# Later blocks' attention bias made by POOL instead of ACT, and the first two weight pieces decoded behind the sixth and seventh pair's exponentials

## The chip, the cores and the metric

The kernel runs on one core of one Trainium2 chip. The metric is device time in microseconds (us), lower is better. Three timed runs of the kernel before gave 570.25, 571.13 and 571.83 us, median 571.13 us. One further execution was profiled; every duration below comes from that one.

The engines are PE (TensorE, matmuls; PEld is its weight load), DVE (VectorE), ACT (ScalarE), POOL (GpSimd) and SP (SyncE, which issues all the DMAs here). Each works through its own instructions in a fixed order and waits for the others by semaphores.

## The reference

Attention with 8 heads of 64 over two batches of 768 tokens, then two dense blocks on the 512-wide result. In the attention every token sees the first few tokens and its own last 96, with a bias that grows with distance, by a slope of its own in each head:

```
scores = q @ k.T / sqrt(D)
dist = where(is_global & ~is_local, n_local, abs(rel))
scores = scores - slopes[h] * dist ; scores = where(keep, scores, -1e9)
a = exp(scores - max) / (sum + 1e-9) ; x = a @ v
x = x + relu(layernorm(x) @ w_ch1) @ w_ch2          # 512 -> 2048 -> 512
theta = x @ w_theta ; y = w_tok_r @ (x cos theta) + w_tok_i @ (x sin theta)
u = x + y ; out = u + relu(u @ w_ch)
```

All inputs are float32 or 64-bit; the weights come in a 64-bit packing and are turned into float32 on the chip ("decoded"), and then split in a high and a low part for the matmuls.

## The kernel before, in words

The 1536 tokens are 12 blocks of 128 rows, taken in the order 0, 6, 1, 2, 3, 4, 5, 7 to 11. Blocks 0 and 6 are the first of their batch: they see only their own 128 columns. Every later block sees a window of 256 columns: 96 earlier ones, 32 for the global tokens, its own 128.

A step of the attention is one pair of heads of one block (four steps to a block). `scores` (L184) gives PE two score matmuls `s`, DVE adds the bias and takes the maximum (L204, tiles `e` and `nm`), and ACT takes the exponential with its sum (L211). Two steps later `flip_probs` transposes `e` on PE into `pt` (L221) and copies it out to `pts`: by ACT for the second and third pair of a block (L224), by DVE for the other two (L226). Three steps later `values` multiplies `pts` with v into `xa` (L240). Six to eight steps later `finish_x` copies `xa` (ACT, L250), transposes it (`xp`, L255) and scales it (DVE, L256), `layer_norm` works on it (DVE and POOL, L268 to L277), and `make_xt` transposes the result (`xnp`, L284). In the first two blocks `spin` puts matmuls of zeros between the steps.

The bias tiles, one of 128 x 384 for each head, are made by `make_bias` (L119) in two parts: `first`, the 128 columns of blocks 0 and 6, and `old`, the 256 columns of all later blocks. DVE builds the distance once (`bias_rel`), and it is scaled once for each head: `first` by DVE (L150), `old` by ACT (L148). The first user of `old` is the third block.

The dense weights come in 58 pieces of 128 x 512. `load_to` (L298) queues the 512 KB load of a packed piece (`raw`) on SP into one of three buffers; `decode` (L306) takes a first approximation on ACT (L314) and three steps on DVE (L322 to L324), and queues the load that may use the buffer next. `split_w` decodes two pieces and makes their high parts on ACT and their low parts on POOL (L340, L341).

The instructions are traced in the order of the code (L768 to L828); a scheduler then settles each engine's order by its own estimate of what is ready first. `tc.issue_after(x)` holds what it encloses, on the engine of x, behind x in that order; it adds no wait for x to end. Around the change the code traces four attention steps, then `split_w(0)` with the first two pieces, then the other steps (L787 to L795). `behind_maximum` (L116) uses `issue_after` for DVE.

Of the kernel before, what the change touches and what calls it, by code (L numbers as in the profile page):

```python
# [8 lines left out]
F32 = mybir.dt.float32  # L9
# [4 lines left out]
AF = mybir.ActivationFunctionType  # L14
ALU = mybir.AluOpType
# [17 lines left out]
def kernel(ctx, tc, q, kwin, v, n_pair, g_ln, wall, out):  # L33
    nc = tc.nc
# [15 lines left out]
    SCALE = 1.0 / D**0.5  # L50
# [13 lines left out]
    def ps(tag, shape, name):  # L64
        return bank(tag, shape, name, BANKS[tag])

    def spin(tag, name, n):

        o = ps(tag, [P, DM], name)
        for _ in range(n):  # L70
            nc.tensor.matmul(o, zero[:, 0:P], zero, start=True, stop=True)
# [11 lines left out]
    def load_n():  # L83
        low = keep.tile([P, 2], F32, name="low")
        nc.vector.tensor_copy(low, words.bitcast(U32)[:, :, 0])
        nc.vector.scalar_tensor_tensor(nval, words[:, :, 1], 2.0**32, low, ALU.mult, ALU.add)
# [24 lines left out]
    nc.vector.memset(zero, 0.0)  # L111
    bias = [at.tile([P, WIN + P], BF16, name=f"bias{h}") for h in range(H)]

    maxima = []

    def behind_maximum(n):  # L116
        return tc.issue_after(maxima[n]) if n is not None else ExitStack()

    def make_bias():  # L119

        n = WIN + P
        rel, key, a = (at.tile([P, n], F32, tag="xn", name=f"bias_{x}", bufs=3) for x in ("rel", "key", "a"))
        io = dict(allow_small_or_imprecise_dtypes=True)
        v_ = nc.vector
        own = rel[:, P:n].rearrange("p (t c) -> p t c", c=P)
        old, first = slice(0, WIN), slice(WIN, n)
        nc.gpsimd.iota(own, [[0, 2], [-1, P]], base=0, channel_multiplier=1, **io)
        nc.gpsimd.iota(key[:, first], [[1, P]], base=0, channel_multiplier=0, **io)
        nc.gpsimd.iota(rel[:, 0:PREV], [[-1, PREV]], base=PREV, channel_multiplier=1, **io)
        nc.gpsimd.iota(key[:, PREV:P], [[1, GLOB]], base=0, channel_multiplier=0, **io)  # L130
        v_.memset(rel[:, PREV:P], FAR)
        v_.memset(key[:, 0:PREV], FAR)
        v_.memset(key[:, P:WIN], FAR)
        v_.tensor_scalar(a[:, P:n], rel[:, P:n], 0.0, FAR, ALU.is_lt, ALU.mult)
        v_.tensor_tensor(rel[:, P:n], rel[:, P:n], a[:, P:n], ALU.max)
        yield
        load_n()
        for part in (first, old):
            r, k_, a_ = rel[:, part], key[:, part], a[:, part]
            with behind_maximum(3 if part is old else None):  # L140
                v_.tensor_scalar(a_, r, nl, NEG, ALU.is_ge, ALU.mult)
                v_.tensor_scalar(k_, k_, ng, NEG, ALU.is_ge, ALU.mult)
            v_.tensor_tensor(r, a_, r, ALU.subtract)
            v_.scalar_tensor_tensor(r, k_, nl, r, ALU.subtract, ALU.max)
            for h in range(H):
                slope = 2.0 ** (-8.0 * (h + 1) / H)
                if part is old:
                    nc.scalar.activation(bias[h][:, part], r, AF.Copy, scale=slope / SCALE)  # L148
                else:
                    v_.tensor_scalar(bias[h][:, part], r, slope / SCALE, None, ALU.mult)  # L150
            yield

    def slot(name):
# [30 lines left out]
    def scores(b, i, p, startup):  # L184
        nk = WIN if i else P
        b0 = 0 if i else WIN
        if p == 0:
            stat[b, i] = (
                at.tile([P, H], F32, tag="nm", name=f"nm{b}_{i}", bufs=2),
                at.tile([P, H], F32, tag="sm", name=f"sm{b}_{i}", bufs=2),  # L190
            )
        nm, sm = stat[b, i]
        qb, kb = qt[b, i], kt[b, i]
        s = [ps("h" if startup and p % 2 else "s", [P, nk], f"s{b}_{i}_{p}_{j}") for j in range(2)]
        k0 = WIN - nk
        for j in range(2):
            rows = slice(j * D, (j + 1) * D)
            nc.tensor.matmul(s[j], qb[rows, p, :], kb[rows, p, k0:WIN], start=True, stop=True)  # L198
        if startup:
            spin("o", f"spin{b}_{p}", 2)  # L200
        e = at.tile([P, 2, nk], F32, tag="p", name=f"e{b}_{i}_{p}", bufs=3)
        for j in range(2):
            h = 2 * p + j
            r = nc.vector.tensor_tensor_reduce(  # L204
                out=e[:, j, :], in0=s[j], in1=bias[h][:, b0:b0 + nk], scale=-SCALE, scalar=3.0e38,
                op0=ALU.add, op1=ALU.min, accum_out=nm[:, h:h + 1],
            )
            maxima.append(r.ins)
        for j in range(2):
            h = 2 * p + j  # L210
            nc.scalar.activation(e[:, j, :], e[:, j, :], AF.Exp, bias=nm[:, h:h + 1], scale=-1.0, accum_out=sm[:, h:h + 1])  # L211
        e_t[b, i, p] = e

    def flip_probs(b, i, p, startup):
# [83 lines left out]
    def load_to(n):  # L298
        while n_staged[0] <= min(n, len(order) - 1):
# [3 lines left out]
            stage[i] = r  # L303
            n_staged[0] += 1

    def decode(i, out):  # L306

        n = n_decoded[0]
        n_decoded[0] += 1
        load_to(n)  # L310
        assert order[n] == i
        r = stage.pop(i)
        load_to(n + NRAW)
        nc.scalar.activation(out, r.bitcast(F32)[:, :, 1], AF.Copy, scale=2.0**-112)  # L314
        t = rawp.tile([P, DM], I32, tag="dec", name=f"dec{i}", bufs=1)
        o = out.bitcast(I32)
        if i >= 4 * GROUP:
            nc.scalar.activation(t, r.bitcast(U32)[:, :, 0], AF.Copy, scale=2.0**-29 * (1 - 2.0**-15), bias=-0.4999)
            nc.vector.scalar_tensor_tensor(t, o, 3, t, ALU.logical_shift_left, ALU.bitwise_or)
            nc.vector.scalar_tensor_tensor(o, r[:, :, 1], -2**31, t, ALU.bitwise_and, ALU.bitwise_or)  # L320
            return
        nc.vector.tensor_scalar(t, o, 3, None, ALU.logical_shift_left)  # L322
        nc.vector.scalar_tensor_tensor(t, o, -2**31, t, ALU.bitwise_and, ALU.bitwise_or)
        nc.vector.scalar_tensor_tensor(o, r[:, :, 0], 29, t, ALU.logical_shift_right, ALU.bitwise_or)  # L324
# [273 lines left out]


    def general():  # L600
        es = ExitStack()
        ga = es.enter_context(tc.tile_pool(name="ga", bufs=1))
        row = ga.tile([P, S], F32, name="g_row")
# [5 lines left out]
        for b in range(B):  # L609
# [3 lines left out]
            for i in range(NQ):  # L613
# [6 lines left out]
                v_ = nc.vector  # L620
# [11 lines left out]
                for h in range(H):  # L632
                    n_ = f"{t}_{h}"
                    e = ga.tile([P, S], F32, tag="e", name=f"g_e{n_}", bufs=2)
                    st_ = ga.tile([P, 3], F32, tag="st", name=f"g_st{n_}", bufs=2)
                    slope = 2.0 ** (-8.0 * (h + 1) / H)
# [82 lines left out]
        for t in range(NTT):  # L719
            o = tmp(f"g_o{t}")  # L720
            nc.vector.scalar_tensor_tensor(o, product(flip(x2[t], f"g_u{t}"), CH, f"g_ch{t}"), 0.0, x2[t], ALU.max, ALU.add)
            b, i = divmod(t, NQ)
# [56 lines left out]
    def steps_to(n):  # L779
        while n_step[0] < n:  # L780
            next(st, None)
            n_step[0] += 1
# [6 lines left out]
    next(bias_steps)  # L789
    load_to(1)  # L790
    nc.sync.dma_start(gbc, g_ln.partition_broadcast(P))
    steps_to(4)
    split_w(0)
    steps_to(done_at(0))
    split_w(1)  # L795
# [75 lines left out]
    with tc.If(nc.values_load(slow[0:1, 0:1], min_val=0, max_val=1, skip_runtime_bounds_check_because="0 or 1") > 0):  # L871
        general()
# [49 lines left out]
```

## Time and profile before

| | |
|---|---|
| timed runs, median (lowest to highest) | 571.13 us (570.25 to 571.83) |
| profiled execution, its whole time | 572.38 us |
| its span, first to last instruction | 570.5 us |
| PE busy in the span | 555.1 us (97%) |
| DVE, ACT, POOL busy | 365.7, 282.7, 121.9 us |
| granted TensorE clock, mean | 0.998 |

The profiled execution took 1.25 us more than the median of the timed runs. PE is busy nearly throughout; an engine's idle time matters only where PE waits for it. The attention of the first blocks fills about the first 60 us, and from there on matmuls of the dense block stand between the attention's steps. Stretches are read from a view that gives each engine's busy time in a window, and waits from a timeline that names, in brackets, how long an engine sat idle before an instruction and what ended that.

### The profile page before, as it was taken

The page shows a single profiled execution, that of the slowest core. Times are in us where ns is not written, and L with a number is a line of the kernel's source. Part 1 is how long each engine was busy: PE and PEld are TensorE (multiplying, and loading weights), DVE is VectorE, ACT ScalarE, POOL GpSimd, SP SyncE. Part 2 cuts the span into 40 slices and gives each one's busy share as a digit, 9 for nine tenths or more (in the row PEclk, how much of TensorE's full clock was granted, in tenths as well). Part 3 has the DMA queues.
Part 4 walks back from the last instruction along what each step waited for, and adds up shares of the span by engine and source line. Part 5 has one row for each costly group of instructions (what it writes and reads, how often), then busy time and mean ns, then how long its engine had stood idle before and what let it go on. Part 6 is the DMA issues. An engine that isn't in the chain of part 4 may idle for free.

```text
span 570.5 us, 9281 instructions
## 1 busy us (share of the span) xinstructions
PE 555.1 (97%) x3531; PEld 461.4 (81%) x3532; DVE 365.7 (64%) x789; ACT 282.7 (50%) x647; POOL 121.9 (21%) x103
## 2 busy tenths in 40 slices
PE   8898999999999999999999999999999999999996
PEld 4465676777888899999989888889888888888885
DVE  6899988857458732278784524462699879871442
ACT  5886864636226511166663415561578777740110
POOL 1455420000002100030300202231033347730000
PEclk9999999999999999999999999999999999999999
DMA  8965655500003410026552000000243200000112
GB/s 262 317 214 187 215 192 204 167 1 2 0 1 109 150 37 1 1 80 198 167 185 74 1 1 1 2 1 0 79 144 132 91 1 1 1 1 1 74 68 86
DMA packets 18548, 49.18 MB, mean 86 GB/s; under 512 B 2240, under 2 KB 4288, under 8 KB 18496
## 3 DMA queue, kind: packets, MB, share of 16 engines
q1 hardware_dynamic: 18496, 48.51, 25.7%
q8 instruction: 30, 0.49, 0.4%
q14 instruction: 22, 0.18, 0.1%
HBM read 45.35 MB, written 3.15 MB: 85 GB/s over the span
## 4 chain that ended last, share of the span: by engine, by line
PE 64%; ACT 1%; DVE 1%; issue 0%; DVEq 0%; ACTq 0%
PE acc L545 17%; PE op L392 17%; PE hp L369 17%; PE thm L480 6%; PE ch L591 6%; PE xp L284 1%; ACT wt L314 0%; ACT xth L285 0%; DVE hl L374 0%; DVE w2l L341 0%; DVE x2all L381 0%; ACT w L314 0%; ACT k L488 0%; ACT k L487 0%; ACT s L493 0%
## 5 line engine op out<-in xcount | busy, mean ns | idle before, releaser
L369 PE MATMUL hp<-xth,w1h 128*128 128x256 f32 x384 | 109.0, 284 | 0.0
L369 PE MATMUL hp<-xth,w1l 128*128 128x256 f32 x384 | 108.7, 283 | 0.0
L369 PE MATMUL hp<-xtl,w1h 128*128 128x256 f32 x384 | 108.4, 282 | 0.0
L374 DVE SCALAR_TENSOR_TENSOR hl<-hp,hh 128x256 fp32r<-128x256 f32 x96 | 40.3, 420 | 79.9 <-ACT hh L373 79.7
L373 ACT ACTIVATE hh<-hp 128x256 fp32r<-128x256 f32 x96 | 36.1, 377 | 95.5 <-PE hp L369 95.5
L545 PE MATMUL acc<-tokh,z 128*128 128x512 f32 (+1 forms) x320 | 79.6, 337 | 0.0
L392 PE MATMUL op<-w2h,hh 128*128 128x512 f32 x192 | 76.9, 401 | 0.7 <-ACT hh L373 0.5
L369 PEld LDWEIGHTS hp<-xth,w1h 128*128 128x128 f32 x384 | 72.6, 189 | 6.1 <-issue 1.5
L369 PEld LDWEIGHTS hp<-xtl,w1h 128*128 128x128 f32 x384 | 72.5, 189 | 5.9 <-issue 1.7
L392 PE MATMUL op<-w2h,hl 128*128 128x512 f32 x192 | 76.1, 396 | 0.0
L392 PE MATMUL op<-w2l,hh 128*128 128x512 f32 x192 | 76.1, 396 | 0.0
L369 PEld LDWEIGHTS hp<-xth,w1l 128*128 128x128 f32 x384 | 72.6, 189 | 1.7 <-issue 1.5
L545 PEld LDWEIGHTS acc<-tokh,z 128*128 128x128 f32 x320 | 55.3, 189 | 7.2
L211 ACT ACTIVATE e<-e,nm 128x256 f32<-128x256 f32 (+1 forms) x96 | 46.2, 482 | 25.3 <-DVE nm L204 23.8
L545 PE MATMUL acc<-tokl,z 128*128 128x512 f32 (+1 forms) x160 | 54.0, 338 | 0.0
L341 POOL TENSOR_TENSOR w1l<-w,w1h 128x512 fp32r<-128x512 f32 x16 | 22.3, 1393 | 136.9 <-ACT w1h L340 136.9
L381 DVE SCALAR_TENSOR_TENSOR x2all<-op,rsall,x2all 128x512 f32<-128x512 f32 x60 | 42.8, 743 | 6.8 <-PE op L392 6.8
L507 POOL TENSOR_TENSOR x2all<-xth,xtl 128x512 f32<-128x512 f32 x12 | 18.3, 1528 | 121.2 <-DVE k L499 116.2
L392 PEld LDWEIGHTS op<-w2h,hl 128*128 128x128 f32 x192 | 36.1, 188 | 9.2 <-DVE hl L374 0.4
L204 DVE CUSTOM_DVE_ANT_0 e<-s,bias 128x256 f32<-128x256 f32 (+1 forms) x96 | 35.5, 393 | 11.6 <-PE s L198 10.9
L457 DVE TENSOR_TENSOR tokl<-wt,tokh 128x512 fp32r<-128x512 f32 x36 | 33.9, 951 | 11.3 <-ACT tokh L456 11.1
L392 PEld LDWEIGHTS op<-w2h,hh 128*128 128x128 f32 x192 | 36.4, 190 | 5.6 <-ACT hh L373 0.7
(155 smaller groups left out, 1072.4 us busy)
## 6 DMA issues: line engine op xcount, KB each, us to landing
raw<-in_wall SPq DMA_DIRECT2D x58, 512.0 KB, 3.3
k<-in_kwin SPq DMA_DIRECT2D x10, 512.0 KB, 5.6
q<-in_q SPq DMA_DIRECT2D x12, 256.0 KB, 4.3
vc<-in_v SPq DMA_DIRECT2D x12, 256.0 KB, 3.3
out<-o SPq DMA_DIRECT2D x8, 256.0 KB, 2.0
vw<-in_v SPq DMA_DIRECT2D x10, 192.0 KB, 2.6
out<-o SPq DMA_DIRECT2D x8, 128.0 KB, 2.0
vw<-in_v SPq DMA_DIRECT2D x10, 64.0 KB, 3.5
```

The source lines that it names most:

```text
L204: r = nc.vector.tensor_tensor_reduce(out=e[:, j, :], in0=s[j], in1=bias[h][:, b0:b0 + nk], scale=-SCALE, scalar=3.0e38, op0=ALU.add, op1=A ...
L211: nc.scalar.activation(e[:, j, :], e[:, j, :], AF.Exp, bias=nm[:, h:h + 1], scale=-1.0, accum_out=sm[:, h:h + 1])
L341: (nc.vector if d and f >= GROUP else nc.gpsimd).tensor_tensor(lo, s, hi.bitcast(F32), ALU.subtract)
L369: nc.tensor.matmul(hp, l, r[:, kk, :], start=(n == 0), stop=(n == 3 * KD - 1))
L373: nc.scalar.activation(hh, hp, AF.Relu)
L374: nc.vector.scalar_tensor_tensor(hl, hp, 0.0, hh.bitcast(F32), ALU.max, ALU.subtract)
L381: nc.vector.scalar_tensor_tensor(x2[t], o, rsall[:, t:t + 1], x2[t], ALU.mult, ALU.add)
L392: nc.tensor.matmul(op_t[c][j], l, r, start=(f == fs[0] and n == 0), stop=(f == fs[-1] and n == 2))
L457: nc.vector.tensor_tensor(lo, src, hi.bitcast(F32), ALU.subtract)
L480: nc.tensor.matmul(mp, l[:, kk, :], r[:, kk, :], start=(n == 0), stop=(n == 3 * KD - 1))
L545: mm = nc.tensor.matmul(o, l[:, dsl], r[:, sl], start=first and not (paired and d % 2), stop=end and not (paired and d % 2 == 0))
L591: nc.tensor.matmul(mp, l[:, kk, es], r, start=(kk == 0 and m == 0), stop=(kk == KD - 1 and m == 2))
```

## The change

It changes four places: (1) `old` is scaled by POOL with a `tensor_scalar` for each head in place of ACT's `activation`; (2) the last exponential of every step is kept in `exps`; (3) the first ACT operation of decoding pieces 0 and 1 is queued behind the exponentials of steps 5 and 6 (counted from 0), the sixth and seventh pair; (4) seven attention steps instead of four are traced ahead of `split_w(0)`.

```diff
-                if part is old:
-                    nc.scalar.activation(bias[h][:, part], r, AF.Copy, scale=slope / SCALE)
-                else:
-                    v_.tensor_scalar(bias[h][:, part], r, slope / SCALE, None, ALU.mult)
+                (nc.gpsimd if part is old else v_).tensor_scalar(bias[h][:, part], r, slope / SCALE, None, ALU.mult)
...
-            nc.scalar.activation(e[:, j, :], e[:, j, :], AF.Exp, bias=nm[:, h:h + 1], scale=-1.0, accum_out=sm[:, h:h + 1])
+            r = nc.scalar.activation(e[:, j, :], e[:, j, :], AF.Exp, bias=nm[:, h:h + 1], scale=-1.0, accum_out=sm[:, h:h + 1])
+        exps.append(r.ins)
...
+    def behind_exponentials(i):
+
+        n = 5 + i if i < 2 else None
+        return tc.issue_after(exps[n]) if n is not None and n < len(exps) else ExitStack()
...
-        nc.scalar.activation(out, r.bitcast(F32)[:, :, 1], AF.Copy, scale=2.0**-112)
+        with behind_exponentials(i):
+            nc.scalar.activation(out, r.bitcast(F32)[:, :, 1], AF.Copy, scale=2.0**-112)
...
-    steps_to(4)
+    steps_to(7)
     split_w(0)
```

On ACT, in the first block (`e_0_2`, `e_0_3`: third and fourth pair) and the second (`e_0_0`, `e_0_1`), with `w` the decoding; the order before:

```order
L148 ACTIVATE bias_99<-bias_rel 128x256
L148 ACTIVATE bias_100<-bias_rel 128x256
L211 ACTIVATE e_0_2_216,sm_0_167<-e_0_2_216,nm_0_166 128x128
L211 ACTIVATE e_0_3_233,sm_0_167<-e_0_3_233,nm_0_166 128x128 x2
L224 ACTIVATE pts_0_1_241<-pt_0_1_238 128x256
L314 ACTIVATE w_246<-raw_204 128x512
L314 ACTIVATE w_256<-raw_206 128x512
L211 ACTIVATE e_0_0_290,sm_0_282<-e_0_0_290,nm_0_281 128x128 x2
L224 ACTIVATE pts_0_2_298<-pt_0_2_295 128x256
L211 ACTIVATE e_0_1_309,sm_0_282<-e_0_1_309,nm_0_281 128x128
L340 ACTIVATE w1h_264<-w_246 128x512
```

and the same place now, from the exponential that stood ahead of the eight bias operations:

```order
L208 ACTIVATE e_0_2_216,sm_0_167<-e_0_2_216,nm_0_166 128x128
L222 ACTIVATE pts_0_1_241<-pt_0_1_238 128x256
L208 ACTIVATE e_0_2_216,sm_0_167<-e_0_2_216,nm_0_166 128x128
L208 ACTIVATE e_0_3_233,sm_0_167<-e_0_3_233,nm_0_166 128x128 x2
L208 ACTIVATE e_0_0_264,sm_0_256<-e_0_0_264,nm_0_255 128x128 x2
L222 ACTIVATE pts_0_2_272<-pt_0_2_269 128x256
L208 ACTIVATE e_0_1_283,sm_0_256<-e_0_1_283,nm_0_255 128x128 x2
L208 ACTIVATE e_0_2_302,sm_0_256<-e_0_2_302,nm_0_255 128x128 x2
L248 ACTIVATE xs_314<-xa_0_243 128x512
L318 ACTIVATE w_324<-raw_204 128x512
L318 ACTIVATE w_334<-raw_206 128x512
```

The eight bias operations are gone, and the two decodings moved from ahead of the second block's first exponentials to behind its sixth and the first block's `xs`.

On SP, the loads of weights (`raw0` to `raw4`) and of the third and fourth block (`q0_2` and `q0_3`, with their k, `vc` and `vw`); before:

```order
L302 DMA raw0_204<-in_wall 128x1024
L302 DMA raw1_206<-in_wall 128x1024
L791 DMA gbc_90<-in_g_ln 128x512
L302 DMA raw2_247<-in_wall 128x1024
L163 DMA q0_2_272<-in_q 128x512
L165 DMA k0_2_273<-in_kwin 128x1024
L174 DMA vw0_2_278<-in_v 96x512
L175 DMA vw0_2_278<-in_v 32x512
L302 DMA raw3_249<-in_wall 128x1024
L170 DMA vc0_2_276<-in_v 128x512
L302 DMA raw4_257<-in_wall 128x1024
```

and now:

```order
L300 DMA raw0_204<-in_wall 128x1024
L300 DMA raw1_206<-in_wall 128x1024
L796 DMA gbc_90<-in_g_ln 128x512
L160 DMA q0_2_246<-in_q 128x512
L162 DMA k0_2_247<-in_kwin 128x1024
L171 DMA vw0_2_252<-in_v 96x512
L167 DMA vc0_2_250<-in_v 128x512
L172 DMA vw0_2_252<-in_v 32x512
L300 DMA raw2_325<-in_wall 128x1024
L160 DMA q0_3_379<-in_q 128x512
L162 DMA k0_3_380<-in_kwin 128x1024
L300 DMA raw3_327<-in_wall 128x1024
```

The third piece's load moved behind all the loads of the third block, the fourth's behind the q and k of the fourth block.

On POOL, between the building of the distances and the first layer norm (`xn`); before:

```order
L129 IOTA bias_rel 128x96
L130 IOTA bias_key 128x32
L341 TENSOR_TENSOR w1l_265<-w_246,w1h_264 128x512
L341 TENSOR_TENSOR w2l_269<-w_256,w2h_268 128x512
L272 TENSOR_SCALAR xn_374<-x2all,mv_371 128x512
```

and now:

```order
L147 TENSOR_SCALAR bias_98<-bias_rel 128x256
L147 TENSOR_SCALAR bias_99<-bias_rel 128x256
L147 TENSOR_SCALAR bias_100<-bias_rel 128x256
L270 TENSOR_SCALAR xn_374<-x2all,mv_371 128x512
L271 TENSOR_TENSOR xn_374<-xn_374,gbc 128x512
L345 TENSOR_TENSOR w1l_343<-w_324,w1h_342 128x512
```

Eight scalings (the last three are shown) stand behind the iotas, and the low parts of the weights come behind the first layer norm.

## Rows read from the trace of the kernel before

**Rows 1.** Page, part 1: busy us (share of the span) xinstructions.

```profile
PE 555.1 (97%) x3531; PEld 461.4 (81%) x3532; DVE 365.7 (64%) x789; ACT 282.7 (50%) x647; POOL 121.9 (21%) x103
```

**Rows 2.** Busy time by stretch: window, length, engines' busy us, clock, DMA share, GB/s.

```profile
11.00:28.40 17.40, 14.82 (x93) 7.88 (x92) 13.79 (x59) 14.81 (x52) 5.89 (x5) 1.00 0.99 318
...
30.00:40.00 10.00, 9.66 (x78) 6.35 (x78) 9.65 (x30) 8.59 (x25) 6.06 (x5) 1.00 0.55 161
40.00:50.00 10.00, 8.69 (x76) 5.90 (x72) 8.58 (x30) 7.68 (x23) 5.16 (x4) 1.00 0.72 256
110.00:120.00 10.00, 10.00 (x66) 8.86 (x66) 6.90 (x14) 2.46 (x7) 0.55 (x1) 1.00 0.16 52
```

**Rows 3.** Timeline of ACT: start us, us, engine, line, op, operands [idle before <-releaser].

```profile
9.65 2.56 ACT L148 ACTIVATE bias<-bias_rel 128x256 bf16<-128x256 f32 x8
12.12 0.39 ACT L211 ACTIVATE e<-e,nm 128x128 f32<-128x128 f32 x1
...
12.51 0.39 ACT L211 ACTIVATE e<-e,nm 128x128 f32<-128x128 f32 x1
...
13.28 0.36 ACT L224 ACTIVATE pts<-pt 128x256 f32<-128x256 f32 x1
14.74 0.67 ACT L314 ACTIVATE w<-raw 128x512 f32<-128x512 f32 x1 [1.11 <-DMA raw<-in_wall]
16.02 0.67 ACT L314 ACTIVATE w<-raw 128x512 f32<-128x512 f32 x1 [0.61 <-DMA raw<-in_wall]
...
17.37 0.36 ACT L224 ACTIVATE pts<-pt 128x256 f32<-128x256 f32 x1
```

**Rows 4.** Timeline of PE.

```profile
10.15 0.27 PE L221 MATMUL pt<-ident,e 128*128 128x128 f32 x1
...
17.78 0.44 PE L240 MATMUL xa<-pts,vc 128*64 128x128 f32 x4 [1.37 <-ACT pts L224]
18.15 0.44 PE L221 MATMUL pt<-ident,e 128*128 128x128 f32 x2
```

**Rows 5.** Timeline of POOL, and of DVE beside it.

```profile
18.72 1.26 POOL L341 TENSOR_TENSOR w1l<-w,w1h 128x512 fp32r<-128x512 f32 x1 [16.63 <-ACT w1h L340]
...
25.62 0.17 DVE L251 TENSOR_SCALAR sm<-sm 128x8 f32<-128x8 f32 x1
...
51.11 1.57 POOL L272 TENSOR_SCALAR xn<-x2all,mv 128x512 f32<-128x512 f32 x1 [4.33 <-DVE mv L269]
...
51.24 0.58 DVE L251 TENSOR_SCALAR sm<-sm 128x8 f32<-128x8 f32 x1
51.74 0.68 DVE L324 SCALAR_TENSOR_TENSOR w<-raw,dec 128x512 int32<-128x512 int32 x1
```

**Rows 6.** Timeline of DVE.

```profile
10.98 0.29 DVE L204 CUSTOM_DVE_ANT_0 e<-s,bias 128x128 f32<-128x128 f32 x1 [0.33 <-PE s L198]
...
16.63 0.69 DVE L324 SCALAR_TENSOR_TENSOR w<-raw,dec 128x512 int32<-128x512 int32 x1
...
19.04 1.49 DVE L323 SCALAR_TENSOR_TENSOR dec<-w,dec 128x512 int32<-128x512 int32 x1
...
28.02 0.42 DVE L204 CUSTOM_DVE_ANT_0 e<-s,bias 128x256 f32<-128x256 f32 x1
```

**Rows 7.** SP's issues, and how long loads of `raw` took in the first 60 us.

```profile
9.26 0.33 SPq L302 DMA_DIRECT2D raw<-in_wall  x1
...
19.00 0.35 SPq L170 DMA_DIRECT2D vc<-in_v  x1
...
DMA to landing us min/median/max: 3.4/5.2/8.9
```

**Rows 8.** ACT's waits for `raw` (total us, times, longest), before 30, 30 to 110; one.

```profile
ACT w L314 <- DMA raw<-in_wall: 1.7, 2, 1.1
...
ACT w L314 <- DMA raw<-in_wall: 6.9, 5, 2.2
...
43.74 0.67 ACT L314 ACTIVATE w<-raw 128x512 f32<-128x512 f32 x1 [1.55 <-DMA raw<-in_wall]
```

More of the change, by code (lines that the diff above doesn't have):

```diff
@@ L112 @@
     bias = [at.tile([P, WIN + P], BF16, name=f"bias{h}") for h in range(H)]
-    maxima = []
+    maxima, exps = [], []
     def behind_maximum(n):
@@ L600, in general @@
     def general():
+        exps.clear()
         es = ExitStack()
```

## The prediction

> **What bounds the kernel now.** I read the page's busy shares first. PE is busy 555.1 of 570.5 us [rows 1], so all that any change of order can return is 15.4 us, and it returns it only where PE stands still. Then the busy time by stretch: from 110 us on PE has stretches without a gap (10.00 of 10.00) [rows 2], in which a lead won earlier is carried through and not used up, because PE has the same work in either kernel. The place of the change is the stretch from 11.0 to 28.4 us, from the second block's first bias operations to the end of the third block's. There, of 17.40 us, PE is busy 14.82, DVE 13.79, ACT 14.81 [rows 2]. No engine is full. They wait for each other in a ring: ACT's exponential, PE's transpose, the copy to `pts`, PE's product with v. What the reader is to see in the timelines is which engine the ring stood for. PE's longest gap, 1.37 us ahead of an `xa` at 17.78, was ended by ACT's copy to `pts` of 17.37 [rows 3, 4]. ACT was late for four reasons that stand in a line on its timeline: eight bias operations (9.65 to 12.12), a wait of 1.11 us for the first raw piece, a wait of 0.61 us for the second, and the two decodings [rows 3].
>
> **The change part by part.**
>
> Bias off ACT. Removed: eight operations that hold ACT from 9.65 to 12.12, 2.47 us [rows 3].
>
> Decoding moved. Removed from that place: the two waits, 1.72 us, and two decodings of 0.67 us [rows 3]. They come back behind the second block's sixth exponential and `xs`. I put that at about 16 us (below), when both pieces have landed (the second by 16.02 [rows 3]), so the waits are gone and the 1.34 us stand later, where ACT has room: of the 17.40 us it idles 2.59 before the change and 2.47 more after it [rows 2, 3].
>
> ACT's and PE's place after both. In the new order the copy to `pts` that PE waited for has in front of it one copy of 0.36 us and five exponentials of 0.39 us each (their starts lie 0.39 apart) [rows 3]. The copy can start when PE's transpose ends, 10.15 + 0.27 = 10.42 [rows 4]. So ACT is through at 10.42 + 0.36 + 1.95 = 12.73 and not at 17.37. But PE does not come there so early: in front of that `xa` the new order has seven groups (two pairs of transposes, another `xa`, two pairs of scores, two spins) behind the `xa` of 11.7, of about 0.37 us each, as the starts 17.78 and 18.15 lie apart [rows 4]: 11.7 + 0.37 + 2.6 = 14.7. PE then does at 14.7 what it did at 17.78, 3.1 us earlier. Two groups of scores that stood in front of it stand behind it now, some 0.4 us and 0.6 us, so like for like PE is 3.1 - 1.0 = 2.1 us ahead. The other way to count gives nearly the same and a ceiling: PE idles 17.40 - 14.82 = 2.58 us in the whole stretch [rows 2]. With ACT out of the way I let 0.4 of it remain (the wait for `xs` before `xp`, and for DVE's bias operation on the first window of 256 columns), so 2.2 us.
>
> DVE. It idles 17.40 - 13.79 = 3.61 us in the stretch [rows 2] and gets no new work. A lead of 2.2 leaves it 1.4 us of slack, so DVE doesn't stop it there; after that it is 9.65 of 10 us busy from 30 to 40 [rows 2], but with the same work as before, so it keeps the lead that it has.
>
> POOL. Added: eight `tensor_scalar` of 128x256. POOL stands idle for 16.63 us up to 18.72 [rows 5], so nothing is queued behind them but the first layer norm (ready at about 20 in the new order) and the low parts of the weights. The trace has no such operation; the nearest is 128x512 in 1.57 us [rows 5]. Bounds: half of that, 0.79, as the columns are half, and the whole 1.57. From 9.65 the eight end at 16.0 or at 22.2. The first user needs only head 0, and the heads of the third block come two by two, from 19 to about 25 us, so even at 1.57 each tile is there first (head 6 at 20.6, head 7 at 22.2); only the layer norm would start 2 us late. I take 0.79 and a price of nothing on the path; the cover is POOL's idle time.
>
> DVE beside POOL. A small `tensor_scalar` of DVE, 0.17 us alone, took 0.58 when a POOL `tensor_scalar` had just begun (51.24 behind 51.11), while a two-input operation in the same POOL span kept its 0.68 [rows 5]. A two-input one took 1.49 and not 0.69 beside POOL's `tensor_tensor` of 18.72 [rows 5, 6]. In the new order there is one small operation of that size in POOL's eight, or two: 0.4 to 0.8 us, inside the 1.4 us of slack. The Trainium skill (SBUF — State Buffer, "Who interferes with whom") states more: whichever of the two starts first holds the shared port pair for its whole instruction and the other fully blocks. The trace agrees for 19.04, not for 51.74. By the rule the change would give back most of its gain, which is one of the rivals (the port).
>
> Weights on SP. Tracing seven steps first moves the third piece's load behind four loads of the third block. It was issued at 9.26; now it stands behind `vc0_2`, which can go only when the first block's products with v are done: 19.00 before [rows 7], about 16 now. A raw load takes 3.4 to 8.9 us, median 5.2 [rows 7], so it lands at 19.4 to 24.9, likely 21.2. ACT comes to its decoding at about 20.8 (it was at 22.3). That is a wait of 0.4 us at the median, none to 4.1 at the ends. Queued behind it on ACT are the third block's next exponentials; PE takes their transposes two steps later, so a wait under 1 us costs nothing. I take 0. For its part, the load that is out of the way brings the third block's q, k and v forward in a stretch where the DMA engines are busy 0.99 of the time [rows 2].
>
> **Sum.** 2.2 us from PE's gaps in this stretch, nothing added, nothing later. 572.38 - 2.2 = 570.2 us for an execution like the profiled one. The median of the timed runs was 571.13, 1.25 lower; on that scale I predict 571.13 - 2.2 = 568.9 us.
>
> **The rivals.**
>
> More comes (over 3.6 us). The later part of the attention has gaps of its own: PE idles 1.31 us from 40 to 50 [rows 2], and ACT waits 6.9 us in five places for raw pieces from 30 to 110, the one at 43.74 for 1.55 us [rows 8]. The new order decodes that piece behind the exponentials of the fifth block's second pair, not ahead of them, so this wait may fall too: 2.2 + 1.3 = 3.5, and up to 2.2 + 2.3 with another 1 us: 566.6. Against it: those orders were settled by the scheduler's estimate, and the loads' times may move just as well the other way.
>
> The lead is given back, within 0.3%. The port: eight POOL operations of 0.79 us back to back, and in the new order DVE has five places with small operations among them (the test of n in three parts, the sums, the reciprocal). Blocked up to one POOL operation each, 5 x 0.79 = 4.0 us, on average half, 2.0: less DVE's 1.4 of slack, 0.6 is lost; at the full 4.0 the lead is gone. Second way to the same end: the DMA engines are at 0.99 [rows 2], so the third to fifth pieces land no sooner, and ACT, ahead by 2.2, waits for them. Either leaves 0.3 to 1.6: 570.1 is the middle.
>
> Slower. The third piece's load is late and ACT stops for it in order. At 8.9 us to landing behind an issue at 16 it is there at 24.9, a wait of 4.1 us; if `vc0_2` goes at 19.00 as before, at 27.9, and the wait is 7.1. Both hold every exponential of the third block, and the fourth and fifth piece's loads, which wait for buffers, behind them. It decides when the wait passes the lead plus the step or so that PE can go on without (2.2 + 1): from 4.1 us on it is +0.9, at 6 about +2.8. Middle +2: 573.1. For it: 8.9 was measured, in this very stretch of full DMA engines. Against: when the load is issued, those in front of it are fewer by itself and the fourth piece.
>
> That the order doesn't do what the change says is excluded by the rows of the order.
>
> **How the numbers follow.** Forecast (1.7 to 3.6 us gained) 0.42; more 0.18; given back 0.28; slower 0.12. The runs differ by 1.6 us, so less than 0.3% (1.7 us) can't be told from no change: faster 0.42 + 0.18 = 0.60, same 0.28, slower 0.12. The forecast's own range is 567.5 to 569.4. The range for 8 in 10 goes down to 566.6, the end of the second case, and up over nearly all of the given-back one, to 571.9.
>
> **What would show it.** Right: ACT's copy to `pts` of the first block's third pair starts near 12.7; PE's `xa` behind it near 14.7 without a gap of over 0.5; PE busy over 0.95 from 11 to 26; the third block's last bias operation, at 28.02 before [rows 6], at about 25.8; eight POOL operations of about 0.8 us from 9.7. Wrong: an ACT wait for `raw` of over 1 us between 19 and 28; small DVE operations of 0.6 us and more between 10 and 16; a lead that is there at 28 us and not at 110.

## The result and the profile after

The changed kernel took 575.75 us (median of 8 executions, 574.19 to 577.66), the kernel before 571.44 us beside it (8 executions, 570.25 to 574.22). The ratio is 1.0073, 95% interval 1.0047 to 1.0100: 0.7% slower and clear of the noise, where 568.9 us was forecast, and outside the range. In every ratio of this document an execution more than 1.5% above the fastest of its kernel is left out, and the medians hold all executions but one, of 769 us at a mean clock of 0.654 (in e4 below). The profiled execution of the changed kernel took 577.66 us with a span of 575.8 us, 5.3 us longer than the span of before. It is the slowest of the eight and has, with 0.986, the lowest mean granted clock (0.986 to 0.994), so what it shows is the effect at its largest.

TensorE's busy time is the first line to read (page, part 1; before in [rows 1]):

```profile
PE 562.9 (98%) x3531; PEld 464.7 (81%) x3532; DVE 366.3 (64%) x789; ACT 280.7 (49%) x639; POOL 129.1 (22%) x111
```

The same 3531 matmuls are busy 562.9 us and not 555.1, 7.8 us more. TensorE's idle time fell from 570.5 - 555.1 = 15.4 us to 575.8 - 562.9 = 12.9, by 2.5 us. That looks like the forecast of 2.2, but it does not show it: e2 below, with as many matmuls, the new order and no fall of the clock, is busy 557.9 of 570.3 us, so its idle time is 3.0 us less for a span only 0.2 us shorter. Busy time in this profile moves with the order too, by 2.8 us in e2 and by 1.5 in e7 (without its zero matmuls), and the rest of the 7.8 us needs another cause. The view by stretch shows it (window, length, busy us of PE, PEld, DVE, ACT and POOL, granted clock, DMA share, GB/s):

```profile
10.00:20.00 10.00, 9.84 (x70) 5.53 (x69) 7.18 (x40) 7.73 (x31) 6.71 (x8) 1.00 1.04 328
20.00:22.00 2.00, 1.74 (x13) 0.88 (x12) 2.00 (x8) 1.48 (x4) 1.20 (x1) 1.00 0.93 320
22.00:24.00 2.00, 0.92 (x4) 0.31 (x3) 2.00 (x6) 1.16 (x4) 1.92 (x3) 0.82 0.96 387
24.00:30.00 6.00, 5.95 (x18) 2.94 (x18) 3.50 (x16) 4.21 (x12) 3.34 (x3) 0.50 0.57 189
30.00:36.00 6.00, 6.00 (x26) 3.98 (x27) 4.19 (x16) 2.97 (x9) 0.37 (x1) 0.50 0.50 177
36.00:40.00 4.00, 4.00 (x35) 2.78 (x32) 2.37 (x6) 2.58 (x8) 4.00 (x4) 0.88 0.43 131
```

and the kernel before in two of these:

```profile
10.00:20.00 10.00, 7.63 (x50) 4.05 (x49) 7.07 (x33) 8.29 (x32) 1.26 (x1) 1.00 1.04 353
...
24.00:30.00 6.00, 5.94 (x40) 3.40 (x39) 5.12 (x22) 5.66 (x19) 3.31 (x3) 1.00 0.89 289
```

From 10 to 20 us TensorE is 2.2 us busier than before. Then it is busy 0.92 of 2 us (22 to 24), and its granted clock falls from 1.00 to 0.50, that is from 2.4 to 1.2 GHz. By the shares, 0.82 and 0.88, it falls at 23.3 and is back at 37.0 us: 13.7 us at half speed. TensorE stands idle for the first 0.7 us of them and then has no gap (11.95 of 12 us from 24 to 36), while DVE and ACT have time to spare. So half of the 13 us in which it worked, some 6.5 us by this estimate, is lost outright. Nothing like it stands in the trace of before, whose clock is 1.00 in all these windows.

The timelines show what led up to it. ACT (start us, us, engine, line, operation, operands, in brackets the idle time ahead and what ended it; before in [rows 3]):

```profile
13.45 0.36 ACT L222 ACTIVATE pts<-pt 128x256 f32<-128x256 f32 x1
...
17.09 1.24 ACT L318 ACTIVATE w<-raw 128x512 f32<-128x512 f32 x2
...
22.84 0.66 ACT L318 ACTIVATE w<-raw 128x512 f32<-128x512 f32 x1 [1.08 <-DMA raw<-in_wall]
23.41 0.49 ACT L208 ACTIVATE e<-e,nm 128x256 f32<-128x256 f32 x1
```

TensorE (before in [rows 4]):

```profile
15.37 0.44 PE L238 MATMUL xa<-pts,vc 128*64 128x128 f32 x4
...
22.22 0.70 PE L195 MATMUL s<-k,q 64*128 64x256 f32 x2
24.05 0.47 PE L219 MATMUL pt<-ident,e 128*128 128x128 f32 x1 [1.13 <-ACT e L208]
24.45 1.22 PE L195 MATMUL s<-k,q 64*128 64x256 f32 x2
```

SP (before in [rows 7]):

```profile
16.59 0.33 SPq L167 DMA_DIRECT2D vc<-in_v  x1
...
17.43 0.42 SPq L300 DMA_DIRECT2D raw<-in_wall  x1
```

POOL and DVE (before in [rows 5, 6]):

```profile
10.53 6.96 POOL L147 TENSOR_SCALAR bias<-bias_rel 128x256 bf16<-128x256 f32 x8 [8.44 <-DVE bias_rel L144]
20.80 1.57 POOL L270 TENSOR_SCALAR xn<-x2all,mv 128x512 f32<-128x512 f32 x1 [3.31 <-DVE mv L267]
22.45 1.44 POOL L271 TENSOR_TENSOR xn<-xn,gbc 128x512 f32<-128x512 f32 x1
...
14.68 0.17 DVE L249 TENSOR_SCALAR sm<-sm 128x8 f32<-128x8 f32 x1
...
20.93 0.83 DVE L326 TENSOR_SCALAR dec<-w 128x512 int32<-128x512 int32 x1
...
22.09 0.68 DVE L327 SCALAR_TENSOR_TENSOR dec<-w,dec 128x512 int32<-128x512 int32 x1
...
23.03 1.41 DVE L328 SCALAR_TENSOR_TENSOR w<-raw,dec 128x512 int32<-128x512 int32 x1
```

Read together: the first decodings wait for nothing and `pts` is copied at 13.45, not 17.37. The third raw piece is issued at 17.43, behind `vc`, as the new order has it, and ACT stands still for it for 1.08 us. Behind it in ACT's order is an exponential, and TensorE waits 1.13 us for that, from 22.92 to 24.05. The clock falls at 23.3, some 0.4 us into this gap: two matmuls of scores that took 0.70 us at 22.22 take 1.22 at 24.45.

The third block's last bias operation on DVE, at 28.02 before [rows 6] and forecast for 25.8, comes at 29.64. The lead from there on can be read from DVE's last bias operation of the last block, which comes last in both kernels, and from two matmuls of the dense block later (the three milestones). Before:

```profile
151.64 0.42 DVE L204 CUSTOM_DVE_ANT_0 e<-s,bias 128x256 f32<-128x256 f32 x1
...
240.03 0.28 PE L369 MATMUL hp<-xth,w1l 128*128 128x256 f32 x1
...
307.58 0.28 PE L369 MATMUL hp<-xth,w1h 128*128 128x256 f32 x1
```

After:

```profile
29.64 0.37 DVE L201 CUSTOM_DVE_ANT_0 e<-s,bias 128x256 f32<-128x256 f32 x1
...
155.81 0.42 DVE L201 CUSTOM_DVE_ANT_0 e<-s,bias 128x256 f32<-128x256 f32 x1
...
244.24 0.28 PE L373 MATMUL hp<-xth,w1l 128*128 128x256 f32 x1
...
312.51 0.28 PE L373 MATMUL hp<-xth,w1h 128*128 128x256 f32 x1
```

The changed kernel is 4.2 us late at 152 and at 240 us, 4.9 at 308, 5.3 at the end. Without the 6.5 us of the clock it would be 6.5 - 4.2 = 2.3 us ahead at 240, by estimate: the forecast's lead. Another 0.7 us goes between 240 and 308, and at the end 6.5 - 5.3 = 1.2 us would be left.

### The profile page after: what moved, and what is told of

Same layout as the page of the kernel before. It is cut to its first block, busy times and chain, and to the rows that moved or that the text cites. A ratio compares the mean times of both kernels' runs of the same rounds, so it can differ in the third digit from the quotient of the medians.

```text
span 575.8 us, 9291 instructions
## 1 busy us (share of the span) xinstructions
PE 562.9 (98%) x3531; PEld 464.7 (81%) x3532; DVE 366.3 (64%) x789; ACT 280.7 (49%) x639; POOL 129.1 (22%) x111
## 4 chain that ended last, share of the span: by engine, by line
PE 47%; DVE 2%; ACT 2%; DMA 2%; issue 1%; ACTq 0%; SPq 0%; DVEq 0%
PE acc L549 17%; PE op L396 9%; PE hp L373 8%; PE thm L484 6%; PE ch L595 6%; DMA raw<-in_wall 2%; DVE dec L323 1%; PE xp L282 1%; ACT dec L322 1%; DVE w L324 1%; DVE thr L324 0%; ACT wt L318 0%; ACT w L318 0%; DVE hl L378 0%; ACT xth L283 0%
## 5 line engine op out<-in xcount | busy, mean ns | idle before, releaser
L201 DVE CUSTOM_DVE_ANT_0 e<-s,bias 128x256 f32<-128x256 f32 (+1 forms) x96 | 35.5, 393 | 17.7 <-PE s L195 15.5
L461 DVE TENSOR_TENSOR tokl<-wt,tokh 128x512 fp32r<-128x512 f32 x36 | 33.9, 952 | 11.4 <-ACT tokh L460 11.2
```

The lines of the kernel that those rows point to most:

```text
L201: r = nc.vector.tensor_tensor_reduce(out=e[:, j, :], in0=s[j], in1=bias[h][:, b0:b0 + nk], scale=-SCALE, scalar=3.0e38, op0=ALU.add, op1=A ...
L461: nc.vector.tensor_tensor(lo, src, hi.bitcast(F32), ALU.subtract)
```

## The experiments

Two theories were set against each other. C: gaps on TensorE make its granted clock fall, and the halved clock is the cost. P: POOL's slower bias operations, and DVE and POOL holding each other up, are the cost, and the clock only goes along. C's number came in e7, e11, e12 and e13, P's in e3, e4, e8 and e9, and neither in e1, e2 and e5. All times are medians, with the lowest and highest; "before" is the kernel before on the same chip in the same session; e1 to e4 ran in one session, e5 to e9 in one, e11 and e12 in one, e13 alone. Where no other kernel is named, the short diffs are against the changed kernel.

The last column counts the executions with a mean granted clock under 0.996. TensorE is done some 5 us before the end in every trace, and the clock is low there (before from 567.8 us on). Half the clock in all of the 5 us would take the mean to 0.996, so a mean under that tells of a fall inside the kernel, and 0.996 or 0.997 can hide a short one. Of the changed kernel all eight are under 0.996.

| run | edit | us | ratio to before, 95% interval | clock under 0.996 |
|---|---|---|---|---|
| e1 | bias on POOL alone | 577.6 (577.1 to 578.0) | 1.0093 [1.0073, 1.0112] | 4 of 4 |
| e2 | order alone | 572.9 (571.3 to 577.1) | 1.0015 [0.9986, 1.0045] | 5 of 10 |
| e3 | after, third piece loaded early | 574.3 (573.0 to 576.7) | 1.0041 [1.0023, 1.0059] | 10 of 10 |
| e4 | after, 16 zero matmuls in block 3 | 576.0 (575.7 to 576.6) | 1.0068 [1.0042, 1.0093] | 1 of 3 |
| e5 | before, none in block 2 | 578.8 (578.3 to 579.5) | 1.0108 [1.0089, 1.0127] | 4 of 4 |
| e7 | e3 and 6 in block 3 | 572.5 (571.5 to 574.3) | 1.0005 [0.9990, 1.0020] | 3 of 10 |
| e8 | e2, third piece loaded early | 573.5 (571.8 to 574.7) | 1.0028 [1.0012, 1.0044] | 4 of 10 |
| e9 | after, 4 in block 3 | 576.1 (574.4 to 576.7) | 1.0053 [1.0036, 1.0069] | 5 of 5 |
| e11 | e7, 4 fewer in block 2 | 571.6 (569.8 to 574.2) | 0.9970 [0.9937, 1.0003] | 3 of 12 |
| e12 | e8 and 4 in block 3 | 572.3 (570.6 to 573.4) | 0.9960 [0.9927, 0.9993] | 0 of 12 |
| e13 | e7, none in block 2 | 571.9 (570.0 to 575.7) | 0.9982 [0.9938, 1.0025] | 4 of 10 |

An edit can also let the scheduler choose another order elsewhere. Apart from the zero matmuls themselves, e12 against e8 and e9 against the changed kernel have the same order on ACT, DVE and POOL; e7 against e3, and e3 against the changed kernel, have it on DVE and POOL, with one decoding earlier on ACT. In e4, e11 and e13 more places differ, and e5 is told below.

**e1 and e2: the two halves of the change.** e1 has neither the binding nor the seven steps; against the kernel before it is:

```diff
-                if part is old:
-                    nc.scalar.activation(bias[h][:, part], r, AF.Copy, scale=slope / SCALE)
-                else:
-                    v_.tensor_scalar(bias[h][:, part], r, slope / SCALE, None, ALU.mult)
+                (nc.gpsimd if part is old else v_).tensor_scalar(bias[h][:, part], r, slope / SCALE, None, ALU.mult)
```

> The bias on POOL alone; the decodings are bound to nothing and four steps are traced ahead of them, as before. Theory C (clock): the changed kernel is slower because TensorE's granted clock was at its lower level (0.50) from 23.3 to 37.0 us, after PE had gaps of 0.2 to 1.1 us between 20 and 24; that costs 13.6 x 0.5 = 6.8 us of PE's work, less the lead of about 2.5 us won before. Here the third piece's load stays where it was, so ACT's wait of 1.1 us for it at 22 is not there: clock 0.997 or 0.998, and a lead of about half the change's, 570 to 571 us. Theory P (POOL and waits): the time was lost to POOL's slower bias (6.96 us, begun at 10.5) and to DVE and POOL holding each other up, and the clock is only along with it: slower than before here too, by 2 to 4 us.

e2 leaves the bias on ACT and has the binding and the seven steps:

```diff
-                (nc.gpsimd if part is old else v_).tensor_scalar(bias[h][:, part], r, slope / SCALE, None, ALU.mult)
+                if part is old:
+                    nc.scalar.activation(bias[h][:, part], r, AF.Copy, scale=slope / SCALE)
+                else:
+                    v_.tensor_scalar(bias[h][:, part], r, slope / SCALE, None, ALU.mult)
```

> The binding of the two decodings and the seven steps alone; the bias stays on ACT. Theory C: the third piece's load is still late, so ACT and then PE wait for it between 20 and 25 us, and the clock falls in most executions: mean clock 0.985 to 0.994, 573 to 577 us. Theory P: no POOL bias, so no loss: 570 to 572 us with whatever clock.

e1 missed theory C's number by far, and P's by 1.7 us, since taking the bias off ACT made the scheduler put the first decoding among the exponentials of the first block. ACT then stood 3.74 us for the raw piece, and TensorE with it:

```profile
14.89 0.67 ACT L311 ACTIVATE w<-raw 128x512 f32<-128x512 f32 x1 [3.74 <-DMA raw<-in_wall]
```

```profile
14.00:16.00 2.00, 0.01 (x1) 1.00 1.02 398
16.00:18.00 2.00, 1.85 (x13) 0.92 1.03 399
18.00:20.00 2.00, 2.00 (x12) 0.50 0.92 294
20.00:24.00 4.00, 4.00 (x14) 0.50 0.58 218
24.00:26.00 2.00, 2.00 (x11) 0.87 0.94 292
```

(The columns are window, length, TensorE's busy time, clock, DMA share, GB/s.) The clock is at 0.50 from 17.7 to 24.5 us behind that gap. Of e1's 5.3 us of span, 3.4 are the clock and about 2 the wait itself. So e1 tells the theories apart only in part: the place where the clock fell moved with the gap. e2 was a draw with the kernel before, and just outside both numbers. Its executions split by mean clock: five at 0.997 or 0.998 took 571.3 to 572.3 us, five at 0.991 to 0.995 took 573.5 to 577.1. Its profiled one, at 0.998, has no fall, though TensorE is busy 0.91 of 2 us from 24 to 26.

**e3: the wait for the third piece taken away.**

```diff
-    load_to(1)
+    load_to(2)
     nc.sync.dma_start(gbc, g_ln.partition_broadcast(P))
```

> The changed kernel with the third piece's load issued right behind the second's. Theory C, if ACT's wait of 1.08 us for that load is what made PE's gap: the gap of 1.13 us at 22.9 shrinks under 0.6, the clock stays at 1.00 from 2 us on, and the time is the one predicted for the change, 568 to 570 us. Theory P: POOL's part is unchanged, so 574 to 576 us.

The wait on ACT is gone and the median is 1.4 us lower, P's number and not C's, since the clock still fell, from 26.8 to 33.6 us, behind another gap:

```profile
23.08 1.41 DVE L328 SCALAR_TENSOR_TENSOR w<-raw,dec 128x512 int32<-128x512 int32 x1
...
24.89 0.70 PE L195 MATMUL s<-k,q 64*128 64x256 f32 x2 [0.80 <-DVE nm L201]
...
152.98 0.42 DVE L201 CUSTOM_DVE_ANT_0 e<-s,bias 128x256 f32<-128x256 f32 x1
```

TensorE waits 0.80 us for DVE, whose `w` operation of 23.08 took 1.41 us and not 0.68 beside POOL's `xn`. So the two theories are not pure rivals: what P describes can open a gap, and what C describes is the price of it. The last bias operation of the attention comes at 152.98 and not at 155.81, 2.8 us earlier, and the shorter fall alone (7.0 us of work in it and not 13) is worth 3.0 by estimate. So by this estimate hardly anything of the changed kernel's wait of 1.08 us was lost as waiting time.

**e4 and e9: the changed kernel with TensorE kept busy by zero matmuls in the third block,** 16 of them, or 4 (with 1 in the place of the last 4):

```diff
-        if startup:
-            spin("o", f"spin{b}_{p}", 2)
+        if startup or (b, i) == (0, 1):
+            spin("o", f"spin{b}_{i}_{p}", 2 if startup else 4)
```

> The changed kernel with four matmuls of zeros more in each step of the third block (16 of about 0.21 us, 3.4 us of PE work that fills gaps in part). Theory C: the clock stays at 1.00 and the 6.8 us come back; the lead of 2.5 less 1 to 3 us for the matmuls that stand in no gap: 569.5 to 572 us, clock 0.997 or more. Theory P: added work on PE can only add: 576 us or more.

> The changed kernel with one zero matmul behind the scores of each head pair of the third block, 4 of 0.21 us instead of the 16 of the earlier run. Theory C: if so little is enough to keep the clock at 1.00, 6.8 us less 0.8: 570.5 to 571.5 us; if it shortens the fall to one of 3.4 or 6.8 us, 572 to 574. Theory P: 576 to 577 us, with the fall of 13.6 us as it was.

With 16 the clock is 1.00 until 38 us: filling the gaps holds it, as C says. But the time did not fall (576.0, at P's bound), since the 16 are 3.4 us of work, and P's mechanism showed itself a little later. Two operations of DVE beside POOL's `xn` and `w1l` took 1.46 and 1.63 us (0.42 and 0.69 alone), TensorE waited 2.55 us for the copy to `pts` behind them, and the clock fell behind that:

```profile
34.23 1.46 DVE L326 TENSOR_SCALAR dec<-w 128x512 int32<-128x512 int32 x1
35.72 1.63 DVE L327 SCALAR_TENSOR_TENSOR dec<-w,dec 128x512 int32<-128x512 int32 x1
...
38.01 0.65 PE L219 MATMUL pt<-ident,e 128*128 128x128 f32 x4 [2.55 <-DVE pts L224]
```

An execution at a mean clock of 1.000 took 575.7 us, so here most of the time went into the added work and such waits and not into the clock.

With 4 the profiled execution has a fall of 6.8 us (27.1 to 33.9) and not of 13.7, and the matmuls that answer to those of 240.03 and 307.58 stand 2.4 and 4.3 us behind them, not 4.2 and 4.9: most of what the clock gave was lost again later. The 4 did not close the gap (TensorE still waits 1.00 us before 24.51), and the mean clocks of the five, 0.989 to 0.994, are those of the changed kernel. C's 572 to 574 was a miss, and 576.1 is P's number.

**e5: the kernel before, without the zero matmuls of its second block.** This is the test from the other side, with nothing of the change in it. Against the kernel before:

```diff
-        if startup:
+        if startup and b == 0:
             spin("o", f"spin{b}_{p}", 2)
```

> The kernel before, without the zero matmuls that its second block issues between its scores (the ones at 15.40 and 20.82 us of its trace and their neighbours, about 8 of 0.21 us). They stand where TensorE is idle 2.4 of 10 us. Theory C (gaps on TensorE lower its granted clock, and the halved clock is what costs): with these gone TensorE stands still longer between 15 and 21 us, its clock falls to 0.50 for 3.4 to 7 us and half of that is lost: 573.5 to 575.5 us. Theory P (work that DVE and POOL do at the same time is what costs; the clock only follows): nothing of that kind changes, the matmuls filled idle time, so 571 to 572 us and a clock of 1.00 throughout.

Eight matmuls of zeros fewer, 1.7 us of work that no result needs, and the kernel is 6.4 us slower, beyond C's number:

```profile
12.00:14.00 2.00, 1.36 (x6) 1.00 1.00 376
14.00:16.00 2.00, 2.00 (x11) 0.53 1.05 399
16.00:18.00 2.00, 1.20 (x8) 0.50 1.03 399
18.00:26.00 8.00, 7.95 (x32) 0.50 0.99 287
26.00:34.00 8.00, 8.00 (x33) 0.50 0.55 186
34.00:36.00 2.00, 2.00 (x10) 0.85 0.08 31
```

The clock is at 0.50 from 14.1 to 34.6 us, 20.5 us. Up to 20 us PE, ACT, DVE and POOL have the same order in both kernels but for the missing matmuls, so at 14.1 P has nothing that could have changed: the fall comes of their absence. All four executions are at a mean clock of 0.980 to 0.985, and of the twenty of before beside them one is. From 21 us on the order differs in places, so the 6.4 us are not the clock's to the last tenth. But TensorE worked 19.65 of those 20.5 us, which at the full clock is 9.8 us less by estimate, more than the whole loss and the 1.7 us together.

**e7: the changed kernel with the early load and six zero matmuls,** two behind the scores of the third block's first three pairs.

```diff
-        if startup:
-            spin("o", f"spin{b}_{p}", 2)
+        if startup or ((b, i) == (0, 1) and p < 3):
+            spin("o", f"spin{b}_{i}_{p}", 2)
...
-    load_to(1)
+    load_to(2)
```

> The changed kernel with the third raw piece loaded right behind the second (as in the run with the early raw load) and two zero matmuls behind the scores of the third block's first three head pairs, 6 of 0.21 us, 1.3 us of TensorE. Theory C: the clock stays at 1.00 through 20 to 40 us, where it was at 0.50 for 6.8 us with the early load alone; that gives back 3.4 us for at most 1.3, so about 2 below the early load alone: 571.5 to 573 us. Theory P: the zero matmuls only add to TensorE, and DVE is as late as it was: 574.3 to 575.5 us.

C's number came, P's did not. TensorE has more matmuls than in e3 and the kernel is 1.8 us faster, 3.3 us faster than the changed one. That is not to be had from a theory in which added work can only add. Seven of its ten executions, at a clock of 0.997 or 0.998, took 571.5 to 573.0 us, and three at 0.991 or 0.992 took 573.9 to 574.3, as e3 does: the fall has become rarer and not impossible. The stretches of the profiled one (all engines, as above) have none:

```profile
20.00:22.00 2.00, 2.00 (x16) 0.98 (x14) 2.00 (x8) 1.60 (x6) 1.75 (x2) 1.00 1.09 251
22.00:24.00 2.00, 1.62 (x10) 0.71 (x6) 1.65 (x5) 0.93 (x5) 2.00 (x2) 1.00 1.00 357
24.00:30.00 6.00, 5.43 (x32) 3.37 (x32) 5.63 (x20) 5.81 (x17) 2.70 (x3) 1.00 0.88 256
30.00:36.00 6.00, 5.60 (x53) 3.48 (x50) 5.69 (x20) 4.86 (x17) 4.58 (x4) 1.00 0.51 174
```

and the three milestones:

```profile
150.16 0.42 DVE L201 CUSTOM_DVE_ANT_0 e<-s,bias 128x256 f32<-128x256 f32 x1
...
238.56 0.28 PE L373 MATMUL hp<-xth,w1l 128*128 128x256 f32 x1
...
306.76 0.28 PE L373 MATMUL hp<-xth,w1h 128*128 128x256 f32 x1
```

At a clock of 1.00 the new order is 1.5 us ahead at 150 and 240 us, with 6 x 0.21 = 1.3 us of zero matmuls in it: up to 2.8 without them, against 2.3 worked out from the changed kernel. By 308 us 0.65 of it is given back.

**e8 and e12: the order alone with the early load, without (e8) and with (e12) four zero matmuls.** Against e2 both have the `load_to(2)` of e3, and e12 has:

```diff
-        if startup:
-            spin("o", f"spin{b}_{p}", 2)
+        if startup or ((b, i) == (0, 1) and p in (1, 2)):
+            spin("o", f"spin{b}_{i}_{p}", 2)
```

> The new order with the later blocks' bias still on ACT, and the third raw piece loaded right behind the second. The order alone took 572.9 us, its undisturbed executions 571.3. Theory C: TensorE's gap of 0.85 us at 25.9 and the short ones before it shrink, because ACT no longer waits for the raw piece; the clock stays at 1.00 in all executions: 570 to 571.5 us. Theory P: DVE's operations beside POOL's (0.83 for 0.42, 1.42 for 0.68) stay where they are and hold the third block: 572 to 573.5 us.

> The new order with the bias on ACT and the early raw load (573.5 us, 571.8 to 574.7), and two zero matmuls behind the scores of the third block's second and third head pair, 4 of 0.21 us. TensorE was busy 0.91 of 2 us from 24 to 26 in it. Theory C: what lay between its fastest and its median was the clock, which fell in some executions after that gap; with it filled all executions lie near the fastest: median 571.5 to 572.3, highest under 573.5. Theory P: the zero matmuls are added work: 574 to 575 us, with the same scatter.

e8 was a miss for C: its executions at a clock of 0.998 and more took 571.8 to 573.0 us, above C's number too, and six of ten lie at 0.995 to 0.997 with 573.2 to 574.7, and 573.5 is P's number. (Two of the six are at 0.997 and took 574.0 and 574.7; whether the clock held these up is not shown.) With the gap at 24 to 26 us filled (2.00 of 2 us in e12, 0.91 in e8) and nothing else changed on ACT, DVE and POOL, all twelve executions have a clock of 0.997 or more and the highest is 573.4: C's number, and not P's.

**e11 and e13: e7 with four, and with all eight, zero matmuls of the second block taken out.** The line of e7 that changes, in e11 and then in e13:

```diff
+            spin("o", f"spin{b}_{i}_{p}", 1 if startup and b else 2)
...
+        if (startup and b == 0) or ((b, i) == (0, 1) and p < 3):
```

> The changed kernel with the early raw load and six zero matmuls in the third block (the version that took 572.5 us), and one zero matmul instead of two behind each pair of scores of the second block: 4 of 0.21 us fewer, in a stretch where TensorE was busy 2.00 of every 2 us. Theory C (gaps on TensorE lower its clock): if TensorE still has no long gap there, the clock stays at 1.00 and the time falls by up to 0.85: 571.5 to 572.3 us; if the four were what kept it up, as the eight were in the kernel before, the clock falls and it is 575 us or more. Theory P (DVE beside POOL is the cost): DVE sets the pace there, 572.5 us as it was.

> The changed kernel with the early raw load and the six zero matmuls in the third block, and none in the second block: the same eight are taken out that cost 6.9 us when they were taken out of the kernel before. Theory C: in the new order TensorE has work of its own there (2.00 of every 2 us busy from 12 to 20 us), so only the short gaps that the eight leave count; if the clock stays at 1.00, 570.5 to 572 us; if the gaps are long enough for it to fall, 574 to 578. A rival (the zero matmuls matter as such, whatever TensorE does beside them): 578 to 579 us, as in the kernel before without them.

Both are C's numbers. The same eight that hold the clock up in the kernel before are hardly needed in the new order, where TensorE has its own work from 10 to 20 us (e13: busy 9.85 of 10 us there, 571.9 us, profiled clock 0.999), though two of e13's ten, at 0.989 and 0.991, took 575.6 and 575.7. Here a zero matmul was worth something only where a gap would be. By the median e11 is the fastest version found. But its interval reaches 1.0003, and it and e12 owe their ratios in part to falls in the kernel before itself: of the 23 executions of before beside them, 10 had a mean clock of 0.992 or less and took 575.9 to 581.0. Where the clock was 0.996 or more, e11's nine have a median of 571.3, e12's twelve 572.3, and the thirteen of before 572.1; e13's six have 570.7, against 572.0 of the ten of before in its session. So what is won is mostly that the clock falls less often; at a full clock no version beats the kernel before by more than 0.3% in the median.

Over the four sessions of the experiments the kernel before ran 75 times: 57 executions with a mean clock of 0.996 or more took 570.1 to 573.3 us, the 14 below 0.99 took 577.2 to 581.0. Of the 14, 12 are from the sessions of e11 to e13, so how often a kernel falls differs from session to session too. The changed kernel's eight all lie between 0.986 and 0.994.

## Why the prediction was wrong

Step by step. *Bias off ACT, decoding moved:* right. ACT's copy to `pts` started at 13.45 (12.7 forecast), TensorE's `xa` at 15.37 (14.7). *The lead:* right at 240 us, 2.2 forecast, 2.3 by estimate from the changed kernel and 1.5 to 2.8 from e7, but only where the clock does not fall. *POOL:* 6.96 / 8 = 0.87 us each (0.79), and no head came late. *DVE beside POOL:* between 10 and 16 us it cost nothing, 0.17 us for the small operation at 14.68; what there was stood in the third block (0.83 for 0.42, 1.41 for 0.68), 1.1 us more in all, in a stretch where DVE was full. The Trainium skill (SBUF — State Buffer, Who interferes with whom) says that a DVE operation with two inputs in SBUF contends with a POOL instruction that reads SBUF; the 1.41 us at 23.03, beside POOL's `xn` of 22.45, agrees. The 0.68 us at 22.09, begun inside POOL's `xn` of 20.80, does not.

The step that failed is the one on the weights, "a wait under 1 us costs nothing. I take 0", and with it the sum's "nothing added, nothing later", which rests on "PE has the same work in either kernel". The wait was 1.08 us, inside its range of none to 4.1 (the load was issued at 17.43 and not at 16), and it was the first of the prediction's own signs of being wrong. As waiting time it did cost about nothing (the estimate from e3). What the sum put at nothing without a reason is the time of TensorE's matmuls: the clock fell in the gap behind the wait, and half speed for 13.7 us cost some 6.5 us, more than the whole lead. The wait is not the only way there: e3 has no such wait, and its clock fell behind another gap. The slower rival had the right place and the wrong mechanism: it asked for more than 2.2 + 1 us before a wait would matter, because it counted waiting time alone. The clock was 1.00 in every row that was read, and a row with TensorE's clock was taken as a constant and not as something that the order of the work can change. The one warning in the trace of before was not read: TensorE issues matmuls of zeros there for no result at all, its gap of 1.37 us at 17.78 [rows 4] went unpunished beside them, and e5 shows that without them the clock falls. A smaller slip: of the 2.47 us of bias operations that the prediction adds to ACT's idle time from 11.0 to 28.4 us, only those from 11.0 to 12.12 lie in that stretch.

A second, smaller step failed too: that a lead is "carried through" where TensorE has no gap. Between 277 and 302 us 0.65 to 1.1 us were given back in e2, e7 and the changed kernel. Before, TensorE has no wait there; in e2 and in the changed kernel it waits for DVE's `hl`, in e2 as here:

```profile
285.51 0.50 PE L399 MATMUL op<-w2h,hl 128*128 128x512 f32 x1 [0.23 <-DVE hl L381]
```

What makes DVE late there was not tested. With this loss the changed kernel would have come out about 1.2 us ahead without the fall, some 570.2 us on the scale of the medians. That is nearly the number of the given-back rival (570.1), but by luck: between 10 and 16 us no small operation was blocked, and the late piece cost next to no waiting time.

What stays open: which gap is enough. The changed kernel fell with 0.92 of 2 us busy; e2's profiled execution did not with 0.91, nor e13's with 0.82, nor the kernel before with 0.63 (16 to 18 us), and executions of one kernel differ. The lag differs too: the clock fell 0.4 us into the gap here, but 1.5 us behind the end of one in e5 and 1.7 us in e1. The runs show that it falls where zero matmuls are taken out of the old order (4 of 4 in e5) and less often where they are put into the new one (10 of 10 in e3, 3 of 10 in e7), not the point from which it happens. A zero matmul also differs in kind from the scores and transposes around it. Whether it is the filled gap or the kind of work that holds the clock, no run separates. The Trainium skill (TensorE: Matmul & The Clock Gate, What's actually happening) says that this gate of the clock has two states and none between; here every stretch inside a fall reads 0.50, and the 0.82 and 0.88 are windows with both.

## What to carry to other kernels

In this kernel a gap on TensorE was not priced by its length: look at the granted clock before and behind it, and ask of every change what gaps it opens, even where the sum of idle time shrinks. Matmuls without a result can be load-bearing; when the order around them changes, they belong where the new gaps are. When busy time and not idle time grew in a trace, read the clock by stretch first, and take a lead from operations that both kernels have and not from sums of idle time.

## What was unexpected of the hardware

In a gap of 1.13 us, behind 12 us of nearly full work (9.84 + 1.74 of 12), the clock fell to half, and it stayed there for 13.7 us although TensorE worked without a break from 24.05 us on; in e5, behind a gap of 0.97 us, for 20.5 us. POOL's eight `tensor_scalar` of 128x256 (0.87 us each, float32 to bfloat16) left DVE's small operations beside them at 0.14 to 0.20 us, while POOL's 128x512 operations stretched DVE's `dec` two to three and a half times (0.42 to 0.83 and 1.46). Which POOL operation it is matters: in the kernel before, up to 80 us, all six two-input operations of DVE's decoding that began inside a POOL `tensor_scalar` of 128x512 kept their 0.68 to 0.69 us (in the changed kernel one took 0.98), while the two begun in the first 0.9 us of a `tensor_tensor` of that size took 1.15 and 1.49.
